# Unit dispatch cut in two halves, and the last whole unit's logits placed ahead of the last convolutions, in a fused convolution and soft-MoE kernel

## The chip, the cores and the metric

The program runs on one core of one Trainium2 chip. The metric is device microseconds of one execution, lower is better; a kernel's time is the median over several executions.

## What is computed

The reference, cut to what matters. A per-head dynamic convolution over 7 taps gives tokens of 192 features; a soft mixture of experts with 8 experts of 4 slots then mixes them.

```python
B, S, D = 8, 3584, 192;  H, K = 8, 7          # N = B*S = 28672 tokens, 32 slots, F = 1024
w = softmax(weight_gen, axis=-1)              # taps, per token and head
out = einsum('bshk,bskhg->bshg', w, x_unf)    # x_unf: 7 shifted windows of x
x = out.reshape(N, D)
logits = x @ phi                              # N x 32
d = softmax(logits, axis=0)                   # over all tokens: dispatch
slot_input = (d.T @ x).reshape(E, 4, D)       # 32 slots
slot_out[e] = relu(slot_input[e] @ w1[e]) @ w2[e]
c = softmax(logits, axis=1)                   # over slots: combine
return c @ slot_out                           # N x 192
```

The softmax over all tokens is done online: a running maximum per slot, and an accumulator that is rescaled whenever the maximum moves.

## The kernel before, in words

The program has three stages on one core. Stage one reads x, makes the convolution, and builds logits and the 32 slot inputs. Stage two runs the experts on the 32 slots. Stage three multiplies the combine weights with the slot outputs and stores 22 MB.

Stage one, where the change lies, works in *slots* k = 0..69. One slot is two pairs of token groups (a group has 104 tokens in 4 blocks of 26). For each slot, `conv(k)` (L266) issues 32 matmuls on TensorE into a PSUM buffer of a ring of three (`banks`, NRING); `conv_out(k)` (L273) copies the result on ScalarE into the token block of the unit, `tms[...]`. `xpose(k)` (L285) transposes those tokens on TensorE into another ring buffer, and `xpose_out(k)` (L291) copies them to `cm`. The convolution's weights are *bands*: per chunk of two slots the softmax over taps runs over `tap_top` (VectorE, L189), `tap_sub` (GpSimd, L197), `tap_exp` (ScalarE, L205), `tap_sum` (GpSimd, L213 to L215), `tap_inv` (VectorE, L219), `tap_mul` (GpSimd, L228 or L232) and `tap_turn` (VectorE, L237).

Four slots make a *unit* of 8 pairs; there are 17 whole units and a final one of 4 pairs (`UNITS`, `final`; slots 68 and 69 belong to it). A unit's token block lives in one of two buffers (NTM = 2), the final one's in `wide`. One unit later the unit's dispatch is done: `logits(u)` (L339, L343) into `ls`; `top(u)` (L349, L351) takes the maximum; `newmax` (a two-pass matmul, L367) and `newmax_out` (L372) make the new running maximum `nm`; `keepmax` (L376) stores it; `dexp` (ScalarE, L380) and `dturn` (VectorE, L400) make the weights `dt`; `dispatch(u)` (L419) multiplies weights with tokens, 16 matmuls into `acb`; `rescale(u)` (L427) folds `acb` into `accS`; `save(u)` (L355) keeps the logits for stage three. A matmul of 32-bit data appears twice in the profile, as two passes.

What sets the order: every step is an `op` with an engine, a cost, what it reads and writes. The order on TensorE and on the DMA queue (SyncE) is the order in which the ops are written; a planner (`model`, `times`) places the other engines' ops by its costs. The written loop is, per slot k, in unit u at position i of four:

```python
convs(k)
if i == 0: xposes(k - 2, k - 1)
elif i == 1: slots(u - 1)                       # logits, top
elif i == 2: settle(u - 1); xposes(k - 2, k - 1)  # newmax ... dturn, fade
elif i == 3: ends(u - 1); saves(u - 1)          # dispatch, rescale, save
```

After the loop stands a tail by hand (v is the last whole unit): the transposes of slot 68, the two half transposes of slot 69 (`xpose_half`, L298, with `half_out`, L304), the maximum and weights of v, the logits of the final unit in three pieces, the two halves of v's dispatch, and the final unit's maximum, weights and dispatch. Stage two begins at L864.

## Time and profile before

| | before |
|---|---|
| time, median of 3 runs | 293.8 us (292.86 to 293.94) |
| the profiled execution: time, span | 294.21 us, 292.2 us |
| TensorE busy, granted clock over the span | 89%, 0.948 |
| VectorE, ScalarE, GpSimd busy | 73%, 62%, 55% |
| HBM read, written | 46.68 MB, 22.36 MB |

The span runs from the first to the last instruction of the profiled execution; some 2 us lie around it. Busy shares are means over three stages with different limits, so they say little by themselves; the stretches have to be read one by one. Matmuls are pipelined, and their ends are modelled, so a busy TensorE is not one at its peak. "issue" as the end of a wait means that nothing the profile shows ended it.

### The profile page before, as it was taken

What the parts mean: (1) busy time and instruction counts of PE and PEld (TensorE: products, weight loads), DVE (VectorE), ACT (ScalarE), POOL (GpSimd) and SP (SyncE); (2) the same over time, 40 slices, a digit from 0 to 9 for tenths busy, and PEclk for the clock granted to TensorE, in tenths of its full rate; (3) what the DMA queues carried; (4) which work ended last, traced back from release to release, by engine and by line L of the source; (5) the groups of instructions that cost most, each with busy time, mean ns of one, the idle gap of its engine ahead of it and who ended that gap; (6) DMA issues with size and microseconds to landing.
All of it is one profiled execution on the core that took longest, in us unless ns stands there. A gap on an engine that the chain in (4) does not pass through costs nothing. (4 is left out here: it accounts for less than half of the span.)

```text
span 292.2 us, 15559 instructions
## 1 busy us (share of the span) xinstructions
PE 259.2 (89%) x6726; PEld 204.4 (70%) x6726; DVE 212.4 (73%) x385; ACT 180.3 (62%) x307; POOL 160.2 (55%) x253
## 2 busy tenths in 40 slices
PE   8699999999999999999999999999999897848510
PEld 4588888888888889889888898898868652312100
DVE  8758997887898787778859696783278598977310
ACT  8768656666676656647665666565322379967430
POOL 9956869478596775657375736630036325473100
PEclk9889999999999999999999999999999999966675
DMA  6866757777677766767676766676798099999993
GB/s 172 239 197 190 210 166 204 224 213 205 192 204 212 210 194 201 209 196 217 176 224 204 208 197 197 186 227 184 239 320 293 28 391 415 417 419 416 417 415 162
DMA packets 30404, 70.06 MB, mean 240 GB/s; under 512 B 5888, under 2 KB 17024, under 8 KB 30336
## 3 DMA queue, kind: packets, MB, share of 16 engines
q1 hardware_dynamic: 30336, 69.07, 72.6%
q8 instruction: 53, 0.87, 1.3%
q14 instruction: 15, 0.12, 0.1%
HBM read 46.68 MB, written 22.36 MB: 236 GB/s over the span
## 5 line engine op out<-in xcount | busy, mean ns | idle before, releaser
L266 PE MATMUL ring<-big,band 128*26 128x96 f32 x4480 | 110.4, 249 | 3.8 <-DVE band L237 2.4
L266 PEld LDWEIGHTS ring<-big,band 128*26 128x26 f32 x4480 | 99.7, 130 | 12.8 <-issue 4.9
L273 ACT COPY tm<-ring 128x768 f32<-128x768 f32 x68 | 54.4, 800 | 60.2 <-PE ring L266 59.8
L237 DVE STREAM_TRANSPOSE band<-wide 128x832 f32<-128x832 f32 x70 | 70.6, 1025 | 4.4 <-POOL wide L228 3.1
L285 PE MATMUL ring<-ident,tm 122*128 122x122 f32 x408 | 50.7, 274 | 0.2 <-issue 0.2
L285 PEld LDWEIGHTS ring<-ident,tm 122*128 122x128 f32 x408 | 44.2, 145 | 2.9 <-POOL si L214 0.3
L228 POOL TENSOR_TENSOR wide<-taps,sum 128x364 f32<-128x364 f32 x32 | 31.4, 981 | 25.6 <-DVE band L237 12.6
L291 ACT COPY cm<-ring 128x624 f32<-128x624 f32 x68 | 44.1, 691 | 2.0 <-PE ring L285 2.0
L197 POOL TENSOR_TENSOR taps<-taps,top 128x364 f32<-128x364 f32 x34 | 33.0, 974 | 5.8 <-DVE top L189 5.5
L213 POOL TENSOR_TENSOR si<-taps 128x208 f32<-128x208 f32 x34 | 21.7, 639 | 20.9 <-ACT taps L205 20.5
L995 PE MATMUL two<-cT,so 32*128 32x442 f32 (+2 forms) x136 | 21.4, 639 | 12.2 <-DVE cT L477 3.8
L189 DVE TENSOR_REDUCE top<-taps 128x52 f32<-128x364 f32 x34 | 27.9, 822 | 3.4 <-DMA taps<-wh 3.1
L95 POOL TENSOR_TENSOR LT<-LT,rm 128x576 f32<-128x576 f32 (+1 forms) x16 | 18.1, 1133 | 17.0 <-DVE rm L93 16.8
L107 POOL TENSOR_TENSOR LT<-LT,sm 128x576 f32<-128x576 f32 (+1 forms) x16 | 18.1, 1133 | 15.1 <-DVE sm L105 15.1
L419 PE MATMUL acb<-tm,dt 128*32 128x193 f32 x544 | 25.6, 327 | 0.1
L995 PEld LDWEIGHTS two<-cT,so 32*128 32x128 f32 x136 | 8.4, 204 | 23.0 <-ACT w1a_sb L1001 7.8
L219 DVE RECIPROCAL sum<-sum 128x52 f32<-128x52 f32 (+1 forms) x36 | 16.4, 455 | 10.8 <-POOL sum L215 10.6
L205 ACT ACTIVATE taps<-taps 128x364 f32<-128x364 f32 (+1 forms) x36 | 18.0, 503 | 7.8 <-POOL taps L197 7.7
L1001 ACT COPY big<-two 128x884 f32<-128x884 f32 (+3 forms) x26 | 17.2, 738 | 4.3 <-issue 3.5
L419 PEld LDWEIGHTS acb<-tm,dt 128*32 128x32 f32 x544 | 16.6, 110 | 3.6 <-DVE dt L400 0.2
L349 DVE TENSOR_REDUCE mx<-ls 128x1 f32<-128x416 f32 x17 | 9.9, 580 | 12.3 <-PE ls L343 12.2
L339 PE MATMUL ls<-cm,phi_sb 128*32 128x416 f32 x136 | 15.8, 512 | 0.0
(137 smaller groups left out, 311.9 us busy)
## 6 DMA issues: line engine op xcount, KB each, us to landing
big<-xh SPq DMA_DIRECT2D x224, 120.0 KB, 3.3
taps<-wh SPq DMA_DIRECT2D x35, 182.0 KB, 3.4
out<-big SPq DMA_DIRECT2D x7, 884.0 KB, 10.0
out<-big SPq DMA_DIRECT2D x6, 936.0 KB, 10.2
w1a_sb<-w1a SPq DMA_DIRECT2D x32, 128.0 KB, 3.4
big<-w2a SPq DMA_DIRECT2D x16, 256.0 KB, 4.1
out<-w1a_sb SPq DMA_DIRECT2D x3, 936.0 KB, 11.5
w1b_sb<-w1b SPq DMA_DIRECT2D x16, 128.0 KB, 3.4
```

What stands on the lines that cost most here:

```text
L95: G.tensor_tensor(out=lt, in0=lt, in1=rms.pop(h).to_broadcast([128, n, NS]), op=ALU.subtract)
L189: V.tensor_reduce(out=row(m), in_=run(c, 0, KT).rearrange("p k s -> p s k"), axis=AX.X, op=ALU.max)
L197: eng.tensor_tensor(out=t, in0=t, in1=rows7(tops.pop((c, 0))), op=ALU.subtract)
L213: eng.tensor_tensor(out=fold, in0=run(c, 0, 4), in1=run(c, 4, 8), op=ALU.add)
L228: eng.tensor_tensor(out=dst, in0=raw[c % NTAP][:, 0:KT], in1=m.unsqueeze(1).to_broadcast([128, KT, n, T]), op=ALU.mult)
L237: V.transpose(bands[c % NBAND][:, b].rearrange("p b j l -> p (b j l)"), wide[:, b].rearrange("p b j -> p (b j)"))
L266: P.matmul(to, bands[g // 8 % NBAND][:, g // 4 % CH, :, i], xbd[:, place(t), :, b * GW : (b + 1) * GW].rearrange("p h (a i) -> p h a i", i ...
L273: copy(tms[tm_at(u)][:, pr + of.start : pr + of.stop, 1 : 2 * D + 1], cv[:, of, 0 : 2 * D])
L285: P.transpose(pt[:, j // 3, o : o + TR], tm[0:TR, pr + j // 3, 1 + o : 129 + o], ident[0:TR, 0:TR])
L291: copy(cm.rearrange("p (a i) (b j) -> p a (i b) j", i=3, j=T), pts["t", k][:, of, 0 : 3 * 128].rearrange("p a (i j) -> p a i j", j=32)[... ...
L419: P.matmul(ac[32 * q : 32 * q + 32], dt[:, g, :], tm[:, g // 2, o : o + D + 1], start=(g < 4), stop=(g + 4 >= 2 * n))
L995: P.matmul(pos[j][q // 2][m * half : m * half + m, q % 2, 0 : n * T], of[32 * q : 32 * q + 32], cT[32 * q : 32 * q + 32, g0 : g0 + n, 0:T] ...
```

## The change

A unit's token block is now two tiles of half the size. Its dispatch is written as two ops: the first half (8 matmuls) stays at position 3 of the next unit; the second half, with the rescale, moves to position 1 of the unit after that, ahead of the next unit's logits. At the end of the loop, the second dispatch half of unit v - 1 and the logits of unit v stand ahead of the last convolution (slot 69) rather than behind it, and v's new maximum, exponential and weights are written before the half transposes of slot 69.

```diff
-    tms = [fix.tile([128, UP, 2 * (D + 1)], F32, name=f"tm{i}") for i in range(NTM)]
+    HU = UP // 2
+    tms = [[fix.tile([128, HU, 2 * (D + 1)], F32, name=f"tm{i}_{j}") for j in range(2)] for i in range(NTM)]
...
-    def ends(u):
-        n = UNITS[u][1]
-        op(TE, 0.17 * n - 0.02, ["dt", *tm_all(u)], ["acb"], dispatch, u)
-        op(VE, 0.4, [("al", u % 2)], ["acb", "accS"], rescale, u)
+    def ends(u, half):
+        op(TE, 0.17 * HU, ["dt", *tm_all(u)[2 * half : 2 * half + 2]], ["acb"], dispatch, u, UP * half, UP * (half + 1))
+        if half:
+            op(VE, 0.4, [("al", u % 2)], ["acb", "accS"], rescale, u)
...
+        if u == final and i == 1:
+            ends(u - 2, 1)
+            slots(u - 1)
         convs(k)
...
-        elif i == 1 and u > 0:
+        elif i == 1 and 0 < u < final:
+            if u > 1:
+                ends(u - 2, 1)
             slots(u - 1)
...
         elif i == 3 and u > 0:
-            ends(u - 1)
+            ends(u - 1, 0)
             saves(u - 1)
     k = SLOTS - 2
+    op(TE, 0.12, ["mq", "mq4", "sel4"], ["acb"], newmax, v)
+    op(VE, 0.2, [], ["acb", ("nm", v % 3)], newmax_out, v)
+    op(PO, 0.2, [("nm", v % 3)], ["mq4"], keepmax, v)
     xposes(k)
+    op(AC, 0.6, [("nm", v % 3)], ["ls", "dd"], dexp, v)
+    for i in range(2):
+        op(VE, 0.43, ["dd"], [("dt", "dth")[i]], dturn, v, UP * i, UP * (i + 1))
+    op(AC, 0.3, [("nm", v % 3), ("nm", (v - 1) % 3)], [("al", v % 2)], fade, v)
...
     halves(0, VE, V.tensor_copy)
-    op(TE, 0.12, ["mq", "mq4", "sel4"], ["acb"], newmax, v)
...
     halves(1, VE, V.tensor_copy)
-    op(AC, 0.6, [("nm", v % 3)], ["ls", "dd"], dexp, v)
...
```

The rest of the diff turns indices into a token block into indices of half a block. No matmul, copy or DMA is added or removed apart from the edge columns of the blocks (eight small memsets in place of four). The list of DMAs on SyncE is the same, row for row. On the other engines the planner made a new order from the first instructions on; three places of the program show what moved.

TensorE near the end of stage one, from the dispatch of unit 15 (v is 16) to the half transposes; `wide` is the token block of the final unit. Before:

```order
L419 MATMUL acb<-tm_87,dt_4323 32x193 x16
L266 MATMUL ring_91<-big,band_84 26x4x3x8 x32
L285 MATMUL ring_92<-ident,tm_86 128x122 x6
L285 MATMUL ring_93<-ident,tm_86 128x122 x6
L266 MATMUL ring_91<-big,band_84 26x4x3x8 x32
L339 MATMUL ls<-cm_4268,phi_sb 32x16x26 x4
L343 MATMUL ls<-cm_4268,phi_sb 32x8x26 x8
L285 MATMUL ring_92<-ident,wide 128x122 x6
L298 MATMUL ring_93<-ident,wide 128x122 x3
L367 MATMUL acb<-mq,sel_106 128x5
L298 MATMUL ring_91<-ident,wide 128x122 x3
```

Changed:

```order
L421 MATMUL acb<-tm_0_88,dt_4327 32x193 x8
L267 MATMUL ring_93<-big,band_84 26x4x3x8 x32
L287 MATMUL ring_94<-ident,tm_1_87 128x122 x6
L287 MATMUL ring_95<-ident,tm_1_87 128x122 x6
L421 MATMUL acb<-tm_1_89,dt_4327 32x193 x8
L341 MATMUL ls<-cm_4271,phi_sb 32x16x26 x4
L345 MATMUL ls<-cm_4271,phi_sb 32x8x26 x8
L267 MATMUL ring_93<-big,band_84 26x4x3x8 x32
L369 MATMUL acb<-mq,sel_108 128x5
L287 MATMUL ring_94<-ident,wide 128x122 x6
L300 MATMUL ring_95<-ident,wide 128x122 x3
L300 MATMUL ring_93<-ident,wide 128x122 x3
```

The whole dispatch of 16 matmuls became two of 8, the second one directly ahead of the logits, and the last convolution (the second L267 of these rows) now follows the logits; v's `newmax` stands ahead of the transposes and no longer between the halves.

GpSimd at the start of stage one, from the first chunk's `tap_sub` to chunk 2's (`si` is the scratch of `tap_sum`, `big` the buffer of x, `ident` the identity for transposes). Before:

```order
L200 TENSOR_TENSOR taps_78<-taps_78,top_1_138 128x7x26
L435 MEMSET big 128x960
L197 TENSOR_TENSOR taps_79<-taps_79,top_0_142 128x364
L435 MEMSET big 128x960
masks.py:197 MEMSET ident 128x128
masks.py:199 AFFINE_SELECT ident<-ident 128x128
L213 TENSOR_TENSOR si<-taps_79 128x208
L214 TENSOR_TENSOR si<-si 128x104
L215 TENSOR_TENSOR sum_0_204<-si 128x52
L232 TENSOR_TENSOR wide<-taps_78,sum_1_162 128x7x26
L197 TENSOR_TENSOR taps_80<-taps_80,top_0_209 128x364
```

Changed:

```order
L201 TENSOR_TENSOR taps_78<-taps_78,top_1_136 128x7x26
L198 TENSOR_TENSOR taps_79<-taps_79,top_0_139 128x364
L437 MEMSET big 128x960 x2
L214 TENSOR_TENSOR si<-taps_79 128x208
L215 TENSOR_TENSOR si<-si 128x104
L216 TENSOR_TENSOR sum_0_163<-si 128x52
L233 TENSOR_TENSOR wide<-taps_78,sum_1_156 128x7x26
L233 TENSOR_TENSOR wide<-taps_79,sum_0_163 128x7x26
masks.py:197 MEMSET ident 128x128
masks.py:199 AFFINE_SELECT ident<-ident 128x128
L198 TENSOR_TENSOR taps_80<-taps_80,top_0_201 128x364
```

The identity left its place ahead of chunk 1's sum and now stands behind the first two `tap_mul`. At the same place VectorE, from chunk 0's first `tap_sum` on (its two halves are done apart). Before:

```order
L211 TENSOR_REDUCE sum_0_148<-taps_78 128x26
L219 RECIPROCAL sum_0_148<-sum_0_148 128x26
L232 TENSOR_TENSOR wide<-taps_78,sum_0_148 128x7x26
L237 STREAM_TRANSPOSE band_83<-wide 128x832
L211 TENSOR_REDUCE sum_1_162<-taps_78 128x26
L219 RECIPROCAL sum_1_162<-sum_1_162 128x26
```

Changed:

```order
L212 TENSOR_REDUCE sum_0_144<-taps_78 128x26
L220 RECIPROCAL sum_0_144<-sum_0_144 128x26
L233 TENSOR_TENSOR wide<-taps_78,sum_0_144 128x7x26
L212 TENSOR_REDUCE sum_1_156<-taps_78 128x26
L238 STREAM_TRANSPOSE band_83<-wide 128x832
L220 RECIPROCAL sum_1_156<-sum_1_156 128x26
```

The second half's sum now stands ahead of the first band's transpose, on which the first convolution waits.

VectorE in the tail, from the copy of slot 68's neighbour to the final unit's maximum. Before:

```order
L291 COPY cm_4268<-ring_93 128x624
L349 TENSOR_REDUCE mx_4459<-ls 128x1
L351 TENSOR_SCALAR mq<-acb,mx_4459 128x4
L304 COPY cm_4451<-ring_93 128x312
L372 TENSOR_REDUCE nm_4484<-acb 128x1
L304 COPY cm_4451<-ring_91 128x312
L400 STREAM_TRANSPOSE dt_4519<-dd 128x256
L349 TENSOR_REDUCE mx_4521<-ring_92 128x1
L351 TENSOR_SCALAR mq<-qneg,mx_4521 128x4
L400 STREAM_TRANSPOSE dt_4519<-dd 128x256
```

Changed:

```order
L293 COPY cm_4271<-ring_95 128x624
L429 SCALAR_TENSOR_TENSOR accS<-accS,al_4377,acb 128x193
L351 TENSOR_REDUCE mx_4455<-ls 128x1
L353 TENSOR_SCALAR mq<-acb,mx_4455 128x4
L374 TENSOR_REDUCE nm_4468<-acb 128x1
L306 COPY cm_4460<-ring_95 128x312
L306 COPY cm_4460<-ring_93 128x312
L402 STREAM_TRANSPOSE dt_4513<-dd 128x256 x2
L351 TENSOR_REDUCE mx_4537<-ring_94 128x1
L353 TENSOR_SCALAR mq<-qneg,mx_4537 128x4
```

Both half copies and both parts of v's `dt` now stand ahead of the final unit's maximum (`mx<-ring`); before, one part of `dt` came behind it.

## Rows read from the trace of the kernel before

**Rows 1.** The page's slices: DMA share in tenths, 40 slices of 7.3 us.
```profile
DMA  6866757777677766767676766676798099999993
```
**Rows 2.** Stretches: us, busy us (count) by engine, granted clock, DMA share, GB/s.
```profile
9.51:11.91 2.40, 0.00 (x0) 0.00 (x0) 1.52 (x2) 2.40 (x4) 2.31 (x5) 1.00 0.87 248
12.80:16.20 3.40, 3.40 (x62) 2.80 (x57) 3.13 (x7) 1.47 (x2) 2.71 (x14) 0.50 0.63 183
20.27:209.50 189.23, 187.56 (x5540) 162.81 (x5543) 147.10 (x253) 121.18 (x207) 115.72 (x188) 1.00 0.70 205
209.50:217.98 8.48, 7.93 (x178) 5.24 (x169) 4.99 (x15) 2.89 (x6) 1.66 (x5) 1.00 0.83 274
240.00:285.00 45.00, 27.22 (x218) 9.11 (x218) 28.09 (x51) 31.04 (x54) 16.82 (x15) 0.78 1.01 416
```
**Rows 3.** Timeline 7 to 18 us: start us, length us, engine line op out<-in.
```profile
7.63 0.52 DVE L211 TENSOR_REDUCE sum<-taps 128x26 f32<-128x208 f32 x1
7.88 0.51 ACT L205 ACTIVATE taps<-taps 128x364 f32<-128x364 f32 x1
...
7.96 1.55 PE L266 MATMUL ring<-big,band 128*26 128x96 f32 x64
...
8.53 0.30 POOL masks.py:199 TENSOR_SCALAR_AFFINE_SELECT ident<-ident 128x128 f32<-128x128 f32 x1
8.79 0.65 POOL L213 TENSOR_TENSOR si<-taps 128x208 f32<-128x208 f32 x1
...
10.81 1.05 DVE L237 STREAM_TRANSPOSE band<-wide 128x832 f32<-128x832 f32 x1
...
11.91 2.17 PE L266 MATMUL ring<-big,band 128*26 128x96 f32 x64 [2.40 <-DVE band L237]
...
14.01 1.48 PE L285 MATMUL ring<-ident,tm 122*128 122x122 f32 x6
...
15.42 1.88 PE L266 MATMUL ring<-big,band 128*26 128x96 f32 x64
...
17.24 0.85 PE L285 MATMUL ring<-ident,tm 122*128 122x122 f32 x6
```
**Rows 4.** Timeline of TensorE's weight loads, stage one.
```profile
29.64 1.19 PEld L419 LDWEIGHTS acb<-tm,dt 128*32 128x32 f32 x32
30.86 1.46 PEld L266 LDWEIGHTS ring<-big,band 128*26 128x26 f32 x64
...
39.96 1.35 PEld L266 LDWEIGHTS ring<-big,band 128*26 128x26 f32 x64 [0.16 <-issue]
...
126.11 0.26 PEld L266 LDWEIGHTS ring<-big,band 128*26 128x26 f32 x9 [0.51 <-issue]
```
**Rows 5.** Timeline of VectorE at 29 us: the two bands of chunk 4.
```profile
29.19 1.97 DVE L237 STREAM_TRANSPOSE band<-wide 128x832 f32<-128x832 f32 x2 [0.20 <-POOL wide L228]
```
**Rows 6.** Timeline 198 to 217 us, the end of stage one.
```profile
198.24 0.88 PE L339 MATMUL ls<-cm,phi_sb 128*32 128x416 f32 x8
...
199.65 1.50 PE L266 MATMUL ring<-big,band 128*26 128x96 f32 x64
...
208.21 1.55 PE L266 MATMUL ring<-big,band 128*26 128x96 f32 x64
...
209.85 0.80 ACT L273 COPY wide<-ring 128x768 f32<-128x768 f32 x1 [1.47 <-PE ring L266]
...
211.77 0.48 PE L298 MATMUL ring<-ident,wide 122*128 122x122 f32 x3
...
213.05 0.48 DVE L304 COPY cm<-ring 128x312 f32<-128x312 f32 x1
...
214.12 0.38 DVE L349 TENSOR_REDUCE mx<-ring 128x1 f32<-128x208 f32 x1
...
214.91 0.36 PE L367 MATMUL ring<-mq,sel 128*128 128x5 f32 x2
...
216.52 0.86 PE L419 MATMUL ring<-wide,taps 128*32 128x193 f32 x16 [0.47 <-DVE taps L400]
```

More of the change, by code (lines that the diff above doesn't have):

```diff
@@ L123, in conv_soft_moe @@
     fold = si[:, 0 : CH * 4 * T].rearrange("p (k j) -> p k j", k=4)
[L125 to L126 removed]
+    HU = UP // 2
+    tms = [[fix.tile([128, HU, 2 * (D + 1)], F32, name=f"tm{i}_{j}") for j in range(2)] for i in range(NTM)]
+    tms.append([wide.rearrange("p b j -> p (b j)")[:, 0 : TAIL * 2 * (D + 1)].rearrange("p (n c) -> p n c", c=2 * (D + 1))])
     dd = fix.tile([128, 2 * UP, 32], F32, name="dd")
@@ L272, in conv_out @@
         cv = pts["c", k]
-        copy(tms[tm_at(u)][:, pr + of.start : pr + of.stop, 1 : 2 * D + 1], cv[:, of, 0 : 2 * D])
+        tm, pr = tms[tm_at(u)][pr // HU], pr % HU
+        copy(tm[:, pr + of.start : pr + of.stop, 1 : 2 * D + 1], cv[:, of, 0 : 2 * D])
     cms = {}
@@ L278, in xpose @@
         u, pr = unit(2 * k)
-        tm = tms[tm_at(u)]
+        tm = tms[tm_at(u)][pr // HU]
         if pr == 0:
@@ L284, in xpose @@
             o = 128 * (j % 3)
-            P.transpose(pt[:, j // 3, o : o + TR], tm[0:TR, pr + j // 3, 1 + o : 129 + o],
+            P.transpose(pt[:, j // 3, o : o + TR], tm[0:TR, pr % HU + j // 3, 1 + o : 129 + o],
                         ident[0:TR, 0:TR])
@@ L298, in xpose_half @@
             P.transpose(pt[:, 0, 128 * j : 128 * j + TR],
-                        tms[tm_at(u)][0:TR, pr + i, 1 + 128 * j : 129 + 128 * j], ident[0:TR, 0:TR])
+                        tms[tm_at(u)][pr // HU][0:TR, pr % HU + i, 1 + 128 * j : 129 + 128 * j], ident[0:TR, 0:TR])
     def half_out(k, i, copy):
@@ L317, in drop @@
             for z in (slice(0, r), slice(r, r + DUP % T)):
-                G.memset(tms[tm_at(u)][z, g // 2, g % 2 * (D + 1) : (g % 2 + 1) * (D + 1)], 0.0)
+                G.memset(tms[tm_at(u)][g // UP][z, g // 2 % HU, g % 2 * (D + 1) : (g % 2 + 1) * (D + 1)], 0.0)
     def fill(n, to):
@@ L418, in dispatch @@
             q, o = g % 4, g % 2 * (D + 1)
-            P.matmul(ac[32 * q : 32 * q + 32], dt[:, g, :], tm[:, g // 2, o : o + D + 1],
+            P.matmul(ac[32 * q : 32 * q + 32], dt[:, g, :], tm[g // UP][:, g // 2 % HU, o : o + D + 1],
                      start=(g < 4), stop=(g + 4 >= 2 * n))
@@ L447, in edges @@
         for u in us:
-            t = tms[u]
-            eng.memset(t[:, :, 0:1], 1.0)
-            eng.memset(t[:, :, 2 * D + 1 : 2 * D + 2], 1.0)
+            for t in tms[u]:
+                eng.memset(t[:, :, 0:1], 1.0)
+                eng.memset(t[:, :, 2 * D + 1 : 2 * D + 2], 1.0)
     def setup():
@@ L717, in conv_soft_moe @@
     halves(0, VE, V.tensor_copy)
-    op(TE, 0.12, ["mq", "mq4", "sel4"], ["acb"], newmax, v)
-    op(VE, 0.2, [], ["acb", ("nm", v % 3)], newmax_out, v)
-    op(PO, 0.2, [("nm", v % 3)], ["mq4"], keepmax, v)
     halves(1, VE, V.tensor_copy)
-    op(AC, 0.6, [("nm", v % 3)], ["ls", "dd"], dexp, v)
-    for i in range(2):
-        op(VE, 0.43, ["dd"], [("dt", "dth")[i]], dturn, v, UP * i, UP * (i + 1))
-    op(AC, 0.3, [("nm", v % 3), ("nm", (v - 1) % 3)], [("al", v % 2)], fade, v)
     op(PO, 0.3, [], tmf, drop, final)
```

1 line of the change is left out of this document (removed).

## The prediction, made before the run

> **What bounds the kernel now.** I read the slices of the page first, then stretches of the three stages, then the timelines of the start, of one unit and of the end of stage one.
>
> The slices show DMA at nine tenths or more only from the 33rd on [rows 1]. The stretches say why: from 240 to 285 us the DMA engines are full (share 1.01, 416 GB/s) [rows 2], and these are the stores. Nothing of the change touches them, so their 45 us move as a block: a microsecond won or lost before the first store is one won or lost at the end.
>
> Stage one is TensorE's. Between 20.27 and 209.50 us it is busy 187.56 of 189.23 us, and all other engines have room, VectorE, the fullest, with 147.10 [rows 2]. A rule of the Trainium skill speaks against that reading: "Trainium Kernel Development and Optimization", section Best Practices, judges how far TensorE is from its limit by MFU and LDWEIGHTS busy, not by matmul busy. By weight loads TensorE would be busy 162.81 of 189.23 us, 86%, and 26 us would be open to a better filling. I go by the waits: the holes in the weight loads are short pauses of 0.16 us when the kind of matmul changes, released by nothing ("issue") [rows 4], and a few holes inside a convolution, such as 0.51 us before 126.11, also released by "issue" [rows 4]. None is a wait for data, so a better spread of the dispatch finds no wait to fill in this stage. Two places are left where order matters: the first 20 us, and the tail from 209.50 us on.
>
> **The change part by part.** The sum is made against the profiled execution: 294.21 us, that is a span of 292.20 and 2.01 around it. It lies 0.41 above the median of 293.8.
>
> *Cut dispatch, 16 units.* A whole block takes 1.23 us from its first weight load to that of the following convolution (30.86 - 29.64) [rows 4]; two halves of 8 matmuls are 2 x 0.61. One more change of kind per unit is added, from dispatch to logits. Its price is not in the trace; the nearest rows are dispatch to convolution, with no hole, and transposes to convolution, with 0.16 us [rows 4]. I take 0, since both neighbours of the new change are 32-column matmuls like those of the first of these rows, and keep 16 x 0.16 = 2.6 us for a rival. Nothing can be gained here, for the same reason. The half blocks cost no wait: half 0 is free when the next unit but one writes it, because its dispatch is two slots older, and half 1's dispatch stands one slot ahead of the copy that overwrites it. The rescale waits for the second half, and what queues behind it on VectorE is a `tap` step or the maximum, which itself waits for the logits behind that half: 0. The eight edge memsets instead of four sit in VectorE time in which it waits for GpSimd: 0; without that cover some 0.1 us.
>
> *The start.* The second convolution waited 2.40 us for its band, which ended at 11.86 (10.81 + 1.05) [rows 3]. That band waits for GpSimd's sum of chunk 1, which began at 8.79 behind the identity (0.30 us, ended 8.83) [rows 3]. Now the identity comes later, and the sum can begin when the exponential is done, at 7.88 + 0.51 = 8.39, say 8.50 [rows 3]: 0.29 us earlier, so the second convolution begins at 11.62. The first one begins later, by the sum of 0.52 us now ahead of its band [rows 3], of which I count 0.45: 8.41 instead of 7.96. It still ends at 9.96, before it is needed. TensorE's idle stretch shrinks from 2.40 to 1.66 us.
>
> *The clock.* After the idle stretch, in which it was still granted 1.00, TensorE had a granted clock of 0.50 from 12.80 to 16.20 us, that is 1.2 GHz instead of 2.4 [rows 2]. The second convolution took 2.17 us, the first transposes 1.48 and the third convolution 1.88 [rows 3], where the first convolution took 1.55 and the next transposes 0.85 at 1.00 [rows 3]. That is 0.62 + 0.63 + 0.33 = 1.6 us. Whether 1.66 us of idle still bring the clock down, no row says; the bounds are 0 and 1.6 us of gain. I take the gain, since the stretch is a third shorter and nothing in stage one that is shorter than the 2.40 us brought it down. With 0.29 the start could give 1.9 us. The next limit is the bands: the two of chunk 4 end at 31.16, the first of them near 30.2, and its convolution began at 30.86 [rows 4, 5], 0.7 us later. They come earlier too, since the new order has ScalarE make their exponential one copy sooner, but I take 0.3 us off: **1.6 us gained**, between 0.3 (the clock falls again) and 1.9.
> The Trainium skill, "TensorE: Matmul & The Clock Gate", section What's actually happening, says that the monitor behind the clock runs free of the kernel's start, so that the moment of a change differs between executions. The spread of the three runs, 292.86 to 293.94, would agree with it, but no run here shows the clock of an execution without profile. By that rule the gain is a matter of chance in each execution, before and after.
>
> *The tail.* The words of the change promise that v's softmax is out of the way when the last convolution ends. What they move ahead, though, is TensorE work: the logits, 1.41 us from their start to that of the convolution behind them (199.65 - 198.24) [rows 6]. The last convolution, at 208.21 before, goes back by it to 209.6, its matmuls end near 211.2, and its copy (0.80 us, 209.85 before) runs from 211.3 to 212.1 [rows 6]. The half transposes, at 211.77 before, wait for that copy and start at 212.2, 0.4 us late; before, the logits covered it. Their two copies on VectorE are in a row, so the second ends near 213.8 instead of 213.53 [rows 6]. Behind them the two parts of v's `dt` (0.45 us each) now come before the final maximum, which starts at 214.6 instead of 214.12; the new maximum's matmul goes from 214.91 to 215.35, and the last dispatch from 216.52 to 217.0 [rows 6]. v's exponential gains nothing, since ScalarE has the copies of both last slots before it. **0.45 us lost.** Bounds: 0.6 lost; and 0.55 gained, if all idle time of TensorE in that stretch (8.48 - 7.93) [rows 2] went.
>
> *DMAs.* The queue's rows are the same. The x buffer that the last convolution reads is given back 1.4 us later; it takes the odd selector, on GpSimd, and parts of the second expert weight matrix, both needed only in stage two: 0.
>
> Sum: 294.21 - 1.6 + 0 + 0.45 = 293.06, **293.1 us**; against the median, -0.25%.
>
> **Rivals.** *The clock falls again* (for it: idle time remains; against: less of it): 294.21 - 0.3 + 0.45 = 294.4. *The tail closes up*: the idle 0.55 us goes, 294.21 - 1.6 - 0.55 = 292.1; with the full 1.9 us, 291.8. For it: the last dispatch has 0.47 us of idle before it, waiting for VectorE [rows 6]; against it: the later copy. *Every added change of kind costs 0.16 us*, slower: at the change from second half to logits, 294.21 + 2.6 - 1.6 + 0.45 = 295.7. It puts the kernel on the slow side of the median from 0.05 us a unit on, and by over 0.5% from 0.14. Against it: no hole between dispatch and convolution. *A hole closes in every unit*, since a half dispatch now fills a place where weight loads paused: 2.6 us less, 290.5. Against it: the holes stand ahead of convolutions and inside the logits, and the change removes none of these places. This is what the rule on LDWEIGHTS busy in the Trainium skill would let one hope for. *The change does nothing that shows*: the bands of the first chunks hold TensorE, and the start's gain and the tail's loss cancel; that lies inside the range of the forecast and of the falling clock, 293.6 to 294.1.
>
> **Chances.** Forecast with its range of 292.2 to 293.9: 0.55. Clock falls: 0.20. Tail closes up: 0.14. Added changes cost: 0.08. A hole closes: 0.03. A measurement of this kernel can tell some 0.5% from no change, that is 292.33 and 295.27 around the median. Faster: the tail's 0.14, the closed holes' 0.03 and 0.05 of the forecast's lower end, 0.22. Slower: 0.08 and 0.02 of the case with the falling clock, 0.10. Same: 0.68. The range reaches from 292.0 to 295.0: it leaves out the lower part of the tail's case (0.06), the closed holes and the added changes, some 0.17.
>
> **What would show it.** Right: the granted clock stays 1.00 from 8 to 20 us, the second convolution starts near 11.6 and the third near 13.9 (15.42 before); the weight loads show no new hole ahead of the logits; the half transposes begin right at the end of a ScalarE copy, and the last dispatch starts some 7.4 us behind the last convolution (216.52 - 208.21 = 8.3 before). Wrong: a clock of 0.50 near 12 us (then 294.4); a hole of 0.1 us or more before every logits block (then the slower rival); half transposes without a wait (then the tail gains); or a wait of TensorE for `dt`, which no row of mine foresees.

## The result, and the profile after

The changed kernel took 295.09 us (median of 20 runs, 294.13 to 298.11) beside 293.95 us for the kernel before (20 runs): 1.0052 of before, 95% interval 1.0030 to 1.0073. A second measurement gave 1.0060 (1.0036 to 1.0085). The ratios, here and below, are estimated from the executions in the faster of a kernel's two states and are not the quotients of the medians (1.0039 here). The forecast was 293.1 us, a shade faster; the change came out slower, by 1.1 to 1.8 us in the medians of the two measurements.

| | before | after |
|---|---|---|
| profiled execution: time, span | 294.21, 292.2 us | 296.26, 294.5 us |
| fourth convolution starts | 18.01 us | 16.06 us |
| last convolution starts (weight loads) | 208.21 us | 212.43 us |
| from there to the first matmul of stage two | 9.77 us | 8.57 us |
| from that matmul to the end | 74.22 us | 73.47 us |

The start went as forecast. The timeline of TensorE after, first five steps of stage one (to be held against [rows 3]):

```profile
8.41 1.55 PE L267 MATMUL ring<-big,band 128*26 128x96 f32 x64 [0.41 <-POOL big L437]
11.49 1.61 PE L267 MATMUL ring<-big,band 128*26 128x96 f32 x64 [1.53 <-DVE band L238]
13.03 0.85 PE L287 MATMUL ring<-ident,tm 122*128 122x122 f32 x6
13.81 1.55 PE L267 MATMUL ring<-big,band 128*26 128x96 f32 x64
```

The second convolution began at 11.49 us after 1.53 us of idle time, no matmul is stretched, and the fourth convolution was 1.95 us ahead of before. All of that, and more, was gone by the last convolution. The stretches after (us, busy us and count by engine, clock, DMA share, GB/s; [rows 2] has before's):

```profile
18.32:212.43 194.11, 190.54 (x5500) 163.90 (x5502) 148.60 (x254) 121.36 (x209) 116.48 (x188) 1.00 0.69 202
212.43:221.00 8.57, 7.96 (x216) 6.01 (x205) 4.75 (x15) 2.79 (x6) 1.61 (x5) 1.00 0.83 258
```

From the fifth convolution to the last one the kernel before needed 208.21 - 20.27 = 187.94 us, the changed one 194.11. Of the 6.17 us more, 1.31 are the logits that now stand ahead of the last convolution. The rest are holes. The undisturbed unit is as long as before (11.33 us), so neither the cut nor the extra change of kind costs TensorE anything by itself.

**Holes of the first kind: the half waits for `dt`.** Unit 6, timeline of all engines. Before (band, newmax, maximum, exponential, `dt`, dispatch):

```profile
96.89 1.03 DVE L237 STREAM_TRANSPOSE band<-wide 128x832 f32<-128x832 f32 x1
...
97.31 0.39 PE L367 MATMUL acb<-mq,sel 128*128 128x5 f32 x2
...
97.85 0.12 DVE L372 TENSOR_REDUCE nm<-acb 128x1 f32<-128x5 f32 x1
...
98.14 0.62 ACT L380 ACTIVATE dd<-ls,nm 128x416 f32<-128x416 f32 x1
...
99.14 0.71 DVE L400 STREAM_TRANSPOSE dt<-dd 128x512 f32<-128x512 f32 x1
...
100.30 0.35 PE L419 MATMUL acb<-tm,dt 128*32 128x193 f32 x4
```

After:

```profile
98.59 0.39 PE L369 MATMUL acb<-mq,sel 128*128 128x5 f32 x2
...
98.69 1.04 DVE L238 STREAM_TRANSPOSE band<-wide 128x832 f32<-128x832 f32 x1 [0.40 <-POOL wide L229]
...
99.65 0.12 DVE L374 TENSOR_REDUCE nm<-acb 128x1 f32<-128x5 f32 x1
...
99.75 0.68 ACT L293 COPY cm<-ring 128x624 f32<-128x624 f32 x1 [0.22 <-PE ring L287]
...
100.33 0.62 ACT L382 ACTIVATE dd<-ls,nm 128x416 f32<-128x416 f32 x1
...
101.23 0.71 DVE L402 STREAM_TRANSPOSE dt<-dd 128x512 f32<-128x512 f32 x1
...
101.99 0.48 PEld L421 LDWEIGHTS acb<-tm,dt 128*32 128x32 f32 x16 [0.42 <-DVE dt L402]
```

Before, the band began ahead of newmax, the maximum came 0.54 us after it, and the exponential 0.83. Now the band waits for GpSimd and begins 0.10 us behind newmax, so the maximum comes 1.06 us after it; on ScalarE a transpose's copy is planned ahead of the exponential, which comes at 1.73; `dt` is done at 3.35 us instead of 2.54. The dispatch's turn is at 2.99. The planner chose this order. With the second half the rescale moved too, from behind the dispatch to just ahead of the maxima (0.41 us of VectorE); that this is why the steps were dealt out anew is likely, but not shown. In units 0 and 3 only ScalarE's copy stands ahead (exponential at 1.73 us), in unit 7 VectorE's other work between exponential and `dt` (done at 3.05). Units 0, 3, 6 and 7 wait so, 1.0 us in all.

**Second kind: the convolution behind the short half waits for its band.** Unit 4, weight loads and VectorE, after:

```profile
77.64 0.71 DVE L402 STREAM_TRANSPOSE dt<-dd 128x512 f32<-128x512 f32 x1
78.28 1.00 DVE L238 STREAM_TRANSPOSE band<-wide 128x832 f32<-128x832 f32 x1
```
```profile
78.41 0.49 PEld L421 LDWEIGHTS acb<-tm,dt 128*32 128x32 f32 x16
79.39 0.73 PEld L267 LDWEIGHTS ring<-big,band 128*26 128x26 f32 x32 [0.50 <-issue]
```

The half takes 0.57 us from its first load to the next convolution when nothing waits; here it is 0.98. The band ends at 79.28, the convolution's first load stands 0.116 us behind. The releaser column says "issue", or in units 0 and 7 ScalarE's copy, but the same 0.114 to 0.116 us stand between the band's end and that load at all twelve such waits in four traces (the change twice, early_maximum and bands_first below). Three waits in the change, in units 0, 4 and 7, 1.3 us.

A whole dispatch takes 1.23 us where the half takes 0.57, so the convolution's turn comes 0.66 us sooner. That alone does not make the band late. The band of the same convolution before (the n-th band in order of time belongs to the n-th convolution), and that convolution's weight loads:

```profile
70.76 1.03 DVE L237 STREAM_TRANSPOSE band<-wide 128x832 f32<-128x832 f32 x1
```
```profile
78.26 1.37 PEld L266 LDWEIGHTS ring<-big,band 128*26 128x26 f32 x57
```

It was done 6.5 us ahead. In units 2 to 8 of the kernel before it is 5.3 to 7.6 us, and only unit 0 is tight, with 0.63; in the change these units have 0.1 to 3.4. So it is the new order, in which the bands are turned later, that used up the room. With the same cut but another order (halves_only below) unit 0 alone waits for a band, 0.14 us.

**Third kind: the logits of v wait for a copy.** The tail after, TensorE and VectorE:

```profile
208.31 1.47 PE L287 MATMUL ring<-ident,tm 122*128 122x122 f32 x12
...
209.71 0.86 PE L421 MATMUL acb<-tm,dt 128*32 128x193 f32 x16
...
210.24 0.81 DVE L293 COPY cm<-ring 128x624 f32<-128x624 f32 x1 [3.90 <-PE acb L421]
...
211.20 0.91 PE L341 MATMUL ls<-cm,phi_sb 128*32 128x416 f32 x8 [0.62 <-DVE cm L293]
```

The copy of the last transposes ends at 211.05, and only half a dispatch (0.57 us) stands between transposes and logits, where a convolution (1.5 us) stood: 0.88 us lost.

**Fourth kind: holes that nothing releases.** At 20.24 and 25.80 us TensorE stood 0.6 and 1.1 us inside a convolution, and again at 61, 71 and 162 us:

```profile
25.80 1.05 PE L267 MATMUL ring<-big,band 128*26 128x96 f32 x38 [0.88 <-issue]
```

To sum such holes, I take all by which the units are longer than 11.33 us, from the fifth convolution to unit 15's newmax, less the waits of the first two kinds: 6.2 us in this execution, 4.4 before. They lie at fixed places of the program; more of them below.

Sum: -1.95 + 1.31 + 1.0 + 1.3 + 0.88 + 1.8 = 4.3, beside the 4.22 us at the last convolution. In the trace of the second measurement the first three kinds stand at the same eight places with the same sizes (0.22, 0.23, 0.48, 0.19; three times 0.48; 0.95 us from one matmul to the next), the fourth kind sums to 2.3. So some 3.2 us of waits for data are the change's own, and the fourth kind is the execution's. So is part of what follows: from the first matmul of stage two to the end, where the program is the same, the traces of all the runs below took 73.3 to 75.1 us, and one 76.4. One execution's time says less than its stage one.

### The profile page after: what moved, and what is told of

It reads as the page before. It is cut to its first block, busy times and chain, and to the rows that moved or that the text cites. A ratio compares the mean times of both kernels' runs of the same rounds, so it can differ in the third digit from the quotient of the medians.

```text
span 294.5 us, 15563 instructions
## 1 busy us (share of the span) xinstructions
PE 262.5 (89%) x6726; PEld 205.6 (70%) x6726; DVE 213.0 (72%) x389; ACT 180.3 (61%) x307; POOL 160.8 (55%) x253
## 4 chain that ended last, share of the span: by engine, by line
PE 79%; DVE 4%; POOL 4%; issue 4%; ACT 4%; POOLq 0%; ACTq 0%
PE ring L267 33%; PE ring L287 15%; PE acb L421 7%; PE two L1002 7%; PE ls L341 4%; PE ls L345 4%; PE ring L914 2%; PE acb L369 2%; ACT big L1008 2%; PE ring L935 1%; POOL big L437 1%; POOL LT L107 1%; DVE cT L479 1%; DVE band L238 1%; ACT w1a_sb L1008 1%
## 5 line engine op out<-in xcount | busy, mean ns | idle before, releaser
L267 PE MATMUL ring<-big,band 128*26 128x96 f32 x4480 | 111.1, 248 | 4.5 <-issue 2.2
L267 PEld LDWEIGHTS ring<-big,band 128*26 128x26 f32 x4480 | 100.3, 130 | 15.0 <-issue 7.5
L287 PE MATMUL ring<-ident,tm 122*128 122x122 f32 x408 | 50.1, 272 | 0.1
L287 PEld LDWEIGHTS ring<-ident,tm 122*128 122x128 f32 x408 | 43.5, 144 | 2.7 <-issue 0.2
L1002 PE MATMUL two<-cT,so 32*128 32x442 f32 (+2 forms) x136 | 23.2, 692 | 11.6 <-DVE cT L479 6.2
L421 PE MATMUL acb<-tm,dt 128*32 128x193 f32 x544 | 29.8, 329 | 0.3 <-DVE dt L402 0.2
L98 ACT ACTIVATE LT<-LT 128x576 f32<-128x576 f32 (+1 forms) x16 | 10.9, 681 | 8.1 <-POOL LT L95 8.1
L341 PE MATMUL ls<-cm,phi_sb 128*32 128x416 f32 x136 | 15.2, 513 | 0.6 <-DVE cm L293 0.6
```

The lines of the kernel that those rows point to most:

```text
L267: P.matmul(to, bands[g // 8 % NBAND][:, g // 4 % CH, :, i], xbd[:, place(t), :, b * GW : (b + 1) * GW].rearrange("p h (a i) -> p h a i", i ...
L287: P.transpose(pt[:, j // 3, o : o + TR], tm[0:TR, pr % HU + j // 3, 1 + o : 129 + o], ident[0:TR, 0:TR])
L341: P.matmul(lp[32 * blk : 32 * blk + 32, lo:hi, :, 0:T], phi_sb[:, 0, :], cm[:, lo:hi, 0:3:2, blk, :], start=True, stop=False)
L421: P.matmul(ac[32 * q : 32 * q + 32], dt[:, g, :], tm[g // UP][:, g // 2 % HU, o : o + D + 1], start=(g < 4), stop=(g + 4 >= 2 * n))
L1002: P.matmul(pos[j][q // 2][m * half : m * half + m, q % 2, 0 : n * T], of[32 * q : 32 * q + 32], cT[32 * q : 32 * q + 32, g0 : g0 + n, 0:T] ...
```

## The experiments

Ratios are to the kernel before, timed on the same chip.

| run | ratio | 95% interval |
|---|---|---|
| tail_only | 1.0031 | 0.9993 to 1.0069 |
| halves_only | 1.0022 | 0.9985 to 1.0059 |
| half_tiles | 0.9997 | 0.9972 to 1.0022 |
| early_maximum | 1.0064 | 1.0028 to 1.0101 |
| bands_first | 1.0089 | 1.0054 to 1.0124 |
| halves_later | 0.9964 | 0.9935 to 0.9993 |
| whole_later | 0.9964 | 0.9940 to 0.9989 |
| halves_after_conv | 1.0063 | 1.0038 to 1.0089 |
| whole_after_conv | 1.0035 | 1.0001 to 1.0069 |
| both_after_conv, later_again | 1.0008, 1.0039 | 0.9977 to 1.0040, 1.0009 to 1.0070 |
| change_again | 1.0060 | 1.0036 to 1.0085 |
| tail_covered | 1.0015 | 0.9988 to 1.0042 |
| tail_whole_covered | 1.0023 | 0.9995 to 1.0051 |
| identity_later | 0.9997 | 0.9957 to 1.0037 |
| identity_by_hand | 0.9991 | 0.9965 to 1.0018 |
| start_by_hand | 0.9954 | 0.9932 to 0.9976 |
| start_and_halves | 0.9980 | 0.9953 to 1.0007 |

**The change taken apart.** tail_only is the kernel before with this (and `newmax` to `fade` of v ahead of the half transposes):

```diff
+        if u == final and i == 1:
+            slots(u - 1)
         convs(k)
...
-        elif i == 1 and u > 0:
+        elif i == 1 and 0 < u < final:
             slots(u - 1)
```

> The kernel before with the change's tail alone: logits of the last whole unit, its row maxima and its exponentials ahead of the last convolution, dispatch whole, token blocks whole. On every engine the order of stage one is that of before up to unit 16, so the start, the clock and the units should read as before. Theory A (the logits have lost their cover): the logits stand right behind the two transposes whose copies they read, and TensorE waits for the VectorE copy: with half a dispatch between them it waited 0.88 us in the changed kernel, with nothing between them 1.4 us; the weight loads of the tail save 0.5 us later. So 294.6 to 295.1 us, 1.002 to 1.004 of before. Rival (the tail is harmless, all of the loss is in the units): 293.7 to 294.1 us, 0.999 to 1.001.

halves_only is the change with that part undone; half_tiles keeps the half tiles alone, with `ends(u - 1)` whole.

> The change without its tail: token blocks in half tiles, the dispatch in two halves a unit apart, the last logits behind the last convolution as before. The planner places GpSimd, VectorE and ScalarE anew, so the start is that of before (2nd convolution at 11.9 us, clock falls). Theory B (an order of VectorE and ScalarE in which the row maximum stands behind a band transposition and the exponentials behind a transpose's copy makes dt late, in units 0, 3 and 6 of the changed kernel): here that order is left in unit 6 alone, so one wait of 0.4 us for dt and one of 0.4 us for a ring buffer, and 294.2 to 294.9 us, 1.001 to 1.003. Rival C (the short first half leaves too little cover in all units, whatever the order): waits of 0.4 us in six units or more, with no gain at the start: 295.8 to 297 us, 1.006 to 1.01.

> The change's token blocks in two half tiles alone: dispatch whole and in its old place, tail old. The planner gives every engine before's order. Theory (the tiles cost nothing, as the waits of each matmul on its block are for a copy long done): the same as before, 293.2 to 294.0 us, 0.998 to 1.002. Rival (more small pieces make the cost): 294.5 us or more, 1.003.

Half tiles are free: every engine has before's order, and the ratio is 0.9997. The other two lose 0.0031 and 0.0022, and each interval alone reaches 1. The sum is near the change's 0.0052, but that is chance in part: neither run has the change's early start, and halves_only has an order of its own, with other waits. Their traces name the places. With the tail alone the line of the logits shows the wait (busy, mean ns, idle):

```profile
L339 PE MATMUL ls<-cm,phi_sb 128*32 128x416 f32 x136 | 15.5, 513 | 1.1 <-DVE cm L291 1.1
```

With the halves alone two halves wait for `dt`, 0.48 and 0.52 us from one matmul to the next, in units 6 and 9: another plan, other units. Rival C (a wait in every unit) falls, theory B was right in kind and wrong in which units.

**VectorE's order by hand.** early_maximum is the change with VectorE's and ScalarE's orders edited behind the planner:

```diff
     at = times({TE: 0.0, VE: 3.2, AC: 4.8, PO: 5.0, SP: 0.7}, TE)
...
+    for u in range(final - 1):
...
+        at[n] = min(at[n], at[m] + 0.15)
...
+        at[x] = min(at[x], at[m] + 0.3)
...
+        at[t] = min(at[t], kept + 0.002)
```

(`m`, `n`, `x` and `t` are newmax, the maximum on VectorE, the exponential and `dt` of unit u; `kept` is the end of at most 1.1 us of other VectorE work; what stood ahead of `n` goes behind it.)

> The changed kernel with one thing moved by hand after the planning: in units 0 to 15 the row maximum nm is first on VectorE after mq, the exponentials stand ahead of the transposes' copies on ScalarE, dt behind at most 1.1 us of other VectorE work; TensorE's order stays word for word. Theory B: the four waits for dt (1.0 us in all, with the pieces inside the half some 1.6) and the waits of the next convolution for a ring buffer (1.3 us) go together, since both hang on the late exponentials: 292.3 to 292.9 us, 0.994 to 0.997 of before. Rival C (the half is too short for the copies): the waits for dt go, the convolutions behind the half still wait 0.4 us each: 293.6 to 294.2 us. Rival D (the loss is TensorE's stalls without a releaser, which no order touches): 295 us, 1.004.

All sixteen `dt` were in time, and the kernel was no faster than the change. VectorE and weight loads in unit 4:

```profile
75.66 0.71 DVE L101 TENSOR_REDUCE sm<-LT 128x18 f32<-128x576 f32 x1
76.29 0.85 DVE L190 TENSOR_REDUCE top<-taps 128x52 f32<-128x364 f32 x1
77.06 1.03 DVE L238 STREAM_TRANSPOSE band<-wide 128x832 f32<-128x832 f32 x1
```
```profile
76.21 0.54 PEld L421 LDWEIGHTS acb<-tm,dt 128*32 128x32 f32 x16
78.21 0.91 PEld L267 LDWEIGHTS ring<-big,band 128*26 128x26 f32 x41 [1.47 <-ACT al L408]
```

What had stood ahead of `dt` now stands ahead of the band, and the convolution waits 1.4 us for it (0.8 in units 0 and 7). Both expectations had named a ring buffer as what it waits for; it is the band. So I turned the band right behind `dt`:

> The run in which the maximum was placed first had dt in time, and its convolutions behind the first half then waited 0.8, 1.4 and 0.8 us, until the band that VectorE had turned behind dt and a softmax or maximum step was done. Here the band of that convolution is turned right behind dt, ahead of that other work; the rest is the same. Theory F (what is short is VectorE's time between the row maximum and the convolution behind the half: 3.57 us from newmax where the whole dispatch gave 4.2, for maximum, dt and a band): both waits go, dt is done by +2.5 us, the band by +3.5, and the time falls to 292.8 to 293.8 us, 0.997 to 1.001. Rival (the work that is pushed back makes the next band or the next unit late): 295 us or more, 1.005.

The band waits fell to 0.3 and 0.4 us (units 5 and 7), but the rival was right: the maxima pushed back were now late for newmax (L369, row from the list of waits; times, longest), and ScalarE's copies for a ring buffer (0.8 us at 79.95).

```profile
PE acb L369 <- DVE mq L353: 1.6, 2, 1.1
```

Both runs start from the change's order, with its late bands. In that order VectorE has no room, up to unit 7, between newmax and the convolution behind the half (3.56 us, 2.99 + 0.57): with `dt` first the band was late, with both first the maxima. It is the order that is short of room rather than VectorE, which is busy 148.60 of 194.11 us. The cut with the bands as far ahead as before was not run.

**The first half one convolution later.**

```diff
         op(TE, 1.4, conv_reads(k), [r], conv, k)
+        u, i = unit(2 * k)
+        if i == 0 and u > 1:
+            ends(u - 2, 0)          # halves_after_conv; ends(u - 2) in whole_after_conv
```

halves_later and whole_later came first; they put the dispatch behind the two transposes that follow. There the convolution's copy has already gone into the same token block, so they multiply `dt` with the next unit's tokens in that place: the same instructions, other numbers. They do not compute the reference's result, and their times only answer the question of the place.

> The halves without the new tail, the first half moved on by one convolution and two transposes (behind the transposes of the next unit's first pieces instead of ahead of them), the second half where it was. dt then has 5.5 us from newmax instead of 3.0; the convolution of the next unit comes 0.57 us sooner after newmax. Theory B (the first half stands too near dt): the two waits of 0.5 us for dt of the run with the halves alone go, and no band is late: 292.8 to 293.5 us, 0.997 to 1.000. Theory F (VectorE's time ahead of that convolution is what is short): the bands are late instead, 294 us or more, 1.002.

> The kernel before with the whole dispatch moved to the same later place, behind the next unit's first convolution and two transposes; whole tiles, old tail. Whether the place or the halving decides: with theory B it is as good as the halves there, 292.5 to 293.5 us, 0.996 to 1.000; if the halving has a cost of its own, it is better than the halves there by 0.5 us or more. Rival: the copies of the next unit's first convolution into the same token block wait for the dispatch, and the transposes behind them: waits of 1 us in each unit and 300 us or more.

Both gave 0.9964, with no wait for `dt`; no cost of the halving shows. On the unit's own tokens the dispatch has to stand ahead of that copy, and the copy then waits for it:

> The halves with the old tail, the first half one convolution later: behind the next unit's first convolution and ahead of the ScalarE copy that writes that convolution into the same half tile, so that the data are those of the change (in the two runs with the later place so far that copy came first, and the dispatch read what it had written: same work, other numbers). dt has 4.3 us from newmax instead of 3.0, the copy stands 0.57 us later. Theory B (the place, 3.0 us behind newmax, is too near for dt in some units): no wait for dt, a few hundred ns for bands or ring buffers, 0.996 to 0.999 of before. Rival F (the copy that now waits for the dispatch, and the bands that are wanted 0.57 us sooner, cost what dt gives back): 1.001 to 1.004, as the halves in the old place.

> The kernel before with the whole dispatch in that place, behind the next unit's first convolution and ahead of its copy. dt has the same 4.3 us; but the copy waits for 1.23 us of dispatch, and the second convolution of the unit, three ring buffers on, comes 1.4 us after it (two sets of transposes), while latency, copy and release take some 1.1 to 1.3: a wait near zero to 0.4 us in each unit if the copy is what binds. Theory B: 0.996 to 1.000. If the half alone fits there: 0.5 us to 3 us more than the halves in this place, 1.000 to 1.006.

> The whole change, its tail too, with the first half in the later place. Stage one has the order of the run with the halves there. Theory A (the new tail costs by itself, as the logits of the last whole unit wait some 0.9 us for a copy): 0.5 to 1.2 us slower than that run without the new tail, 0.998 to 1.002 of before. Rival (the tail only moved work and its loss came from the units): the same as without the new tail.

With the later place no first half waits for `dt` any more (its turn is 4.31 us behind newmax, `dt` done by 3.7 at the latest); whole_after_conv has one such wait, 1.2 us in unit 10. The times fit no theory as a whole: halves with the old tail 1.0063, the whole dispatch 1.0035, halves with the new tail 1.0008. One part can be read: with the old tail the halves add 1.0 us behind the last convolution (10.81 us to stage two, 9.77 before), 0.57 of it the second half of unit 15 that stands there now; with the new tail it is 8.58, and with the 1.31 of the moved logits 9.89. So the new tail suits the halves better than the old one. Why halves_after_conv is as slow as it is beyond that stays open; of the 2.5 us by which its trace is longer than that of both_after_conv, 1.3 lie behind the start of stage two (75.07 against 73.76 us), where the two programs do not differ. On one chip with the change:

> The changed kernel as it is, beside the next run on the same chip. If the loss is real and not a matter of the chip: 1.003 to 1.007 of before, as measured first (1.0052). Rival (its first time was made by a few late instruction blocks of TensorE, which differ from run to run): 0.999 to 1.003.

> The whole change with the first half behind the next unit's first convolution, once more. Theory B (3.0 us behind newmax is too near for dt and for the band of the next convolution): 0.003 to 0.006 below the change on the same chip, 0.998 to 1.002 of before. Rival (place is indifferent): within 0.002 of the change.

1.0060 and 1.0039. The two measurements of either kernel together put the later place some 0.3% below the change; taken singly their intervals overlap.

**The tail covered.** In tail_covered unit 15's first half moves next to its second, between transposes and logits; in tail_whole_covered the whole dispatch of unit 15 does, on the kernel with the tail alone.

> The kernel of the run before with one move: the first half of unit 15 is not behind the convolution but behind the two transposes, next to the second half, so that 1.1 us of dispatch stand between the last transpose and the last whole unit's logits instead of 0.57. Theory A (those logits wait for the last VectorE copy of a transpose): the wait of 0.5 to 0.6 us falls to 0 to 0.1, and the time by 0.4 to 0.6 us: 0.997 to 1.000 of before. Rival (the wait passes to the next thing, the row maxima behind the logits): the same time as the run before.

> The kernel before with the change's tail, as in the run with the tail alone, but the whole dispatch of unit 15 moved from ahead of the last convolutions to between the two transposes and the last whole unit's logits. Theory A: the 1.33 us wait of those logits falls to 0 to 0.1, the logits of stage one are as before, and the new tail's 0.0 to 0.1 us net remain: 0.998 to 1.001 of before, 0.003 below the tail alone (1.0031). Rival (the tail loses elsewhere, behind the logits): 1.002 to 1.004.

The wait is gone in both traces; the line of the logits in tail_whole_covered:

```profile
L339 PE MATMUL ls<-cm,phi_sb 128*32 128x416 f32 x136 | 15.0, 513 | 0.0
```

In time it hardly shows. tail_whole_covered is 0.0008 below tail_only; tail_covered is 0.0024 below later_again but 0.0007 above both_after_conv. Both ratios lie above the ranges of theory A, which end at 1.000 and 1.001; the differences are less than these measurements can tell.

**The start alone.** identity_later adds a read of the first chain's products to `make_identity`'s op; identity_by_hand and start_by_hand leave the plan and move single steps in it. start_by_hand:

```diff
     at = times({TE: 0.0, VE: 3.2, AC: 4.8, PO: 5.0, SP: 0.7}, TE)
...
+    at[mul] = at[nth(tap_inv, 0, HI)] + 0.01            # mul = nth(tap_mul, 0, HI)
+    at[nth(tap_turn, 0, HI)] = at[mul] + 0.01
+    at[ident_op] = at[nth(tap_sum, 1)] + 0.01
+    at[nth(tap_top, 2)] = at[nth(tap_inv, 1)] + 0.01
+    at[nth(tap_sub, 2)] = at[nth(tap_mul, 1, HI)] + 0.01
```

> The kernel before with one planning rule changed: GpSimd makes the identity only after the first chain's products, so that the band of the 2nd convolution is turned some 0.5 us sooner; all else is before's, dispatch whole, tail old. Theory E (the changed kernel's early start is worth its gain by itself, with the clock): 2nd convolution at 11.4 us, 4th at 16.1 us where before has 18.0, clock full from there, and 292.0 to 292.8 us, 0.994 to 0.996. Rival (an early start is handed back, as TensorE then meets later bands or a stall without a releaser): 293.4 to 294.1 us, 0.998 to 1.001.

> The kernel before with one step moved by hand after planning: GpSimd makes the identity behind the product of the first chain's second half instead of ahead of the sums before it. All else is before's order. GpSimd's product then stands 0.5 us sooner, the 2nd convolution at 11.4 us instead of 11.9. Theory E (the early start and the clock are worth their time when no unit pays for them): clock full at the start, 4th convolution at 16.1 us instead of 18.0, and 1.0 to 1.9 us less: 0.994 to 0.997 of before. Rival (before's clock falls only in part of its executions, so that its median holds half of it already, or later bands take it back): 0.997 to 1.000.

> The kernel before with the start ordered by hand, the units untouched: the first chain's second product and its band go first on GpSimd and VectorE, ahead of the second chain's sums; the identity behind those sums; the third chain's maximum and subtraction behind the second chain's. The 2nd convolution can start at 10.2 us instead of 11.9 if its data are in, TensorE's idle time before it falls from 2.4 us to 0.7, and the clock has no reason to fall. Theory E: 4th convolution at 15 to 15.5 us, and 1.5 to 2.7 us less: 0.991 to 0.995 of before. Rival (the bands of the next convolutions, or late instruction blocks, take it back): 0.995 to 1.000.

> The same start by hand on the kernel with the halves later, the new tail and its logits covered (1.0015 of before as it was, with a start and a fall of the clock like before's). If the start's gain adds to it: 0.993 to 0.997 of before. If the halves and the tail give anything beside it, this is below the same start on the kernel before; by the runs so far they give nothing, and it should be 0.001 to 0.003 above it.

identity_later kept the clock and had the fourth convolution at 16.14 us, but its new plan made unit 11 wait 1.1 us for `dt`: no gain. identity_by_hand left 2.15 us of idle time, and the clock fell all the same (0.56 and 0.59 from 12 to 16 us). start_by_hand, TensorE's timeline:

```profile
7.88 1.55 PE L266 MATMUL ring<-big,band 128*26 128x96 f32 x64 [0.50 <-DVE band L237]
10.44 1.61 PE L266 MATMUL ring<-big,band 128*26 128x96 f32 x64 [1.00 <-DVE band L237]
...
13.05 1.56 PE L266 MATMUL ring<-big,band 128*26 128x96 f32 x64 [0.22 <-DVE band L237]
...
15.44 1.55 PE L266 MATMUL ring<-big,band 128*26 128x96 f32 x64
...
18.30 1.55 PE L266 MATMUL ring<-big,band 128*26 128x96 f32 x64 [0.54 <-DVE band L237]
```

One microsecond of idle time, no fall, the fourth convolution 2.6 us ahead of before, the units' order untouched: 0.9954, 290.60 us beside 292.26, on the border between the two expectations. The fifth convolution waits for its band and is 1.97 us ahead of before.

At 18.30 us it is also level with the change's fifth (18.32, clock 1.00 in both). So this run is the change's start with the units and the tail of before, and no dispatch and no convolution in its units waits for `dt` or a band. It is 0.0098 to 0.0106 faster than the change, some 3 us, though measured on another chip. The traces agree: stage two begins at 214.27 us here, at 221.00 and 217.10 in the two traces of the change; less what lengthens the units without a wait for data (2.7, 6.2 and 2.3 us) these are 211.6, 214.8 and 214.8. The 3.2 us between them are the sum of the waits counted above.

The same start on the kernel with the later halves and the covered tail gives 0.9980, which is 0.0026 more; the two intervals overlap.

## Why the prediction was wrong

**The start: right.** Forecast: second convolution at 11.62 us, third near 13.9, clock full, 1.6 us gained. Measured: 11.49, 13.81, clock 1.00, 1.95 in the profiled execution, a shade above the bound of 1.9. Its worth in the median is smaller, since before does not always lose it: of twelve traces whose start has before's order on GpSimd and VectorE, eight show the fall (2.22 to 2.52 us of idle time, fourth convolution near 18.0); three with 1.79 to 2.06 us, in which the first convolution began later, do not (fourth convolution at 16.5), nor does one with 2.46. An estimate from these twelve is 8/12 x 1.95 + 4/12 x 0.4 = 1.4 us; with 3.2 us of waits against it the change should lose some 1.8, and lost 1.1 to 1.8. The forecast weighed a rule of the Trainium skill, "TensorE: Matmul & The Clock Gate", section What's actually happening, by which the moment of a change is a matter of chance in each execution. The trace with 2.46 us agrees with it; the other eleven are sorted by the length of the idle time alone.

**The cut dispatch: the step that failed.** The term was 0; it cost some 2.3 us (1.0 for `dt`, 1.3 for bands). "None is a wait for data" was true of before, and from it I took "Nothing can be gained here" as if it also said that nothing could be lost. The added change of kind did cost nothing, as forecast. Nor did a hole close: weight loads fill 84% of the stretch after the change (163.90 of 194.11 us), 86% before. What the term took for granted is that the other engines keep their order in the units. Of the rescale it says "what queues behind it on VectorE is a `tap` step or the maximum, which itself waits for the logits behind that half: 0", and that asks only about the next step. That step was not late, but the planner dealt out all steps anew, and in its order `dt` and the bands are done later. The dispatch's turn is 2.99 us behind newmax in both kernels, but `dt` of unit 6 is done at 3.35 instead of 2.54; the band of unit 4's convolution is done 0.1 us ahead of it instead of 6.5. Only then does the shorter half matter: the three late bands end 3.83 to 4.03 us behind newmax, where the convolution's turn is at 4.13 behind a whole dispatch and at 3.48 behind a half. I had counted slack for the start (a band with 0.7 us to spare, [rows 4, 5]) and not for the units, and had compared the new order at three places, none of them in the units. Whether the cut would be free in an order with early bands was not run; halves_only, whose bands are earlier, still waits 1.1 us. The forecast's own test, "a wait of TensorE for `dt`, which no row of mine foresees", is what the trace showed; rows of before that would have foreseen it exist: in units 9 and 12 `dt` was done 0.08 and 0.14 us ahead of its dispatch.

**The tail: right in kind, too small.** Forecast 0.45 us lost, bound 0.6. Behind the last convolution it went better than said: the last dispatch 6.9 us after it (7.4 forecast), 0.1 us lost net of the moved logits. Ahead of it the logits waited 0.88 us, since I moved them by their length alone and did not ask which copy they now stood right behind.

**The rivals.** None named this cause. "Every added change of kind costs" had the right sign and size (295.7) for the wrong reason.

## What to carry to other kernels

With a planner that deals out the other engines' work anew, the trace of before no longer tells their order: this change moved bands on VectorE by several microseconds, in units where it only seemed to cut a step of TensorE. So write down for each feeder of TensorE (here `dt`, the bands, the copies), unit by unit, when it is done and when its reader's turn comes, in the old order and in the new one; busy shares show nothing of it. A block of matmuls between a feeder and its reader is cover, and to shorten it costs what the feeder's slack does not hold: here nothing where a band was 6 us ahead, and 0.14 us where it had 0.63. A gain at one place is best had by moving single steps with the rest of the order held, as start_by_hand did.

## What the runs showed of the hardware

TensorE's holes without a releaser lie a multiple of some 253 of its instructions apart. The page after lists 6726 matmuls, as many weight loads, and this queue:

```profile
q8 instruction: 53, 0.87, 1.3%
```

13452 / 53 = 254 instructions for each packet of 16 KB. In the change the packet that fits the hole at 25.80 started at 23.52 us and took 0.98, among transfers that kept the DMA engines full (from 23.3 to 24.6 us this queue had 4.7% and the loads 93.0%); the hole ended 1.3 us after it, as others did (1.2 to 1.5). So the holes look like instructions that arrive late behind the kernel's own loads. No run took this apart. With the same order on TensorE the same places stand in the traces with other sizes: near 160 us 0.7, 1.0 and 0.9 us in the kernel before, half_tiles and tail_only, and their sums, taken as above, were 4.4, 3.6 and 5.0 us. Differences of that size are of the order of the spread between executions (292.6 to 296.8 us before).

A late load can cost twice. In identity_by_hand VectorE waited 3.0 us for weights at 59.93, newmax waited 1.8 us for the maximum, and then the clock fell in mid-stage. Timeline and stretches:

```profile
59.93 0.88 DVE L189 TENSOR_REDUCE top<-taps 128x52 f32<-128x364 f32 x1 [3.03 <-DMA taps<-wh]
...
62.64 0.36 PE L367 MATMUL acb<-mq,sel 128*128 128x5 f32 x2 [1.80 <-DVE mq L351]
```
```profile
60.60:62.60 2.00, 0.25 (x12) 0.05 (x4) 1.97 (x5) 0.80 (x1) 1.25 (x3) 1.00 0.77 243
62.60:64.60 2.00, 1.96 (x14) 1.99 (x14) 2.00 (x5) 1.01 (x2) 0.83 (x2) 0.71 0.63 183
64.60:66.90 2.30, 2.30 (x54) 1.99 (x57) 1.99 (x3) 1.04 (x3) 0.33 (x1) 0.51 0.42 132
66.90:69.00 2.10, 2.10 (x84) 1.76 (x75) 0.18 (x1) 1.40 (x3) 0.25 (x1) 1.00 0.54 135
```

Granted 0.51 from 64.6 to 66.9 us, that is 1.2 GHz, and full again from 66.9: the wait of 1.8 us was followed by more than 3 us at a lower clock.
